# What a list scheduler charges for one pass of a split product beside its columns

## The chip, the cores and the metric

The kernel runs on one core of one Trainium2 chip. The metric is the device time of one execution in microseconds (us). The engines are TensorE (PE; its weight loads are listed as PEld), VectorE (DVE), ScalarE (ACT), GpSimd (POOL) and SyncE (SP), which issues all DMAs of the work described here from one queue, in order. Each engine executes its own instructions in the order in which the program was written out.

## The reference

The input is `q`, `k`, `v` (4 batches, 12 heads, 448 positions, 64 columns each, float32) and six weight matrices. What is computed:

```
attn = softmax(causal(q @ k^T / 8)) @ v          # per batch and head, 448 x 448 scores
x    = attn as 1792 tokens x 768
h    = ((x @ w1) * (x @ w2)) @ w3                # w1, w2: 768 x 1024, w3: 1024 x 1024
x2   = h @ w_out                                 # 1024 x 768
h2   = x2 @ w_in                                 # 768 x 2048
out  = (h2 - tanh(h2)) @ w_out2                  # 2048 x 768
```

## The kernel before

**Split products.** Every large product is computed with both operands split into a high part (rounded to the matmul's format `fp32r`) and a low part (the rest). One step over 128 rows of the contraction is three matmuls into the same PSUM tile: high x low, low x high, high x high. They stand in `gemms` (lines 411, 412 and 413), and one such triple is called a split product here, each of its matmuls a pass. The 896 tokens of a half are worked in two blocks, of 384 and of 512 columns (`BLOCKS`); a 128-column tile of weights is the stationary operand. `w3 @ w_out` is multiplied first (`product`, 384 columns in each pass), so that the bilinear layer is followed by one projection.

**Stages.** The first half of the tokens is batches 0 and 1, the second half batches 2 and 3. `attention` (first half) works 12 pairs of heads: scores (L488), masked minimum (L459, DVE), exponentials (L501, ACT), transposes of the probabilities (L513), their evacuation to SBUF (L267), the product with `v` (L541), the transposed reciprocals (L548), scaling and splitting (L552, L554, L267, L270). `turned` (second half) does the same in another layout (scores L657, product with `v` L683). Beside both run the conversions of the weights (`convert`: load L295, then L304, L314, L317, L321, the high part by a copy L267, the low part by a subtraction L270, the store L327), the product `w3 @ w_out`, and the bilinear layer and the projection of the first half. After the attention come the bilinear layer and the projection of the second half, beside the rest of the conversions, and then the last two layers for both halves (`Second`), with weight tiles fetched (L375) from the scratch that the conversions stored: 768-column tiles into the ring `hl` of three buffers, 512-column tiles into the ring `w`.

**What sets the order.** The program is written out by a list scheduler, `Plan`, when the kernel is built. Each piece of work is a generator (a flow) that asks for an engine and a duration, for a buffer of a ring, or for an event. `Plan.run` keeps the time at which each engine comes free (`free`), takes among all flows the request that can start first (then the lower rank, then the one that was ready first), adds its charge to the engine's time, and lets the flow emit its instructions there. A request may name several engines (`[act(n), dve2(n)]` for a copy, `[pool(n), dves(n)]` for a subtraction); then the one that would end first is taken, with VectorE handicapped by 1.5 us (1.0 us after the attention). The charges are the small functions at lines 198 to 233: `act`, `dve`, `pool`, `pe`, `wide`, `dma`.

All large products of a stage come from one flow with rank `FILLER` = 1000, one after the other; the attention's flows have ranks from 0 up. An attention step that asks for PE and whose last step was on another engine is treated as ready 0.5 us (`MARGIN`) later than it is. So products are placed on PE until an attention step is due. The ends of all requests also decide when evacuations, conversions and DMAs are placed on their engines.

`pe` is called in three places: for a split product, `pe(n, 3)` with n = 384 or 512 (L410); for the transposes of the probabilities, `pe(112, count, 112)` (L508); and for the transposes of the reciprocals, `pe(112, 4, 128)` (L546). The scores and the products with `v` are charged by `wide` or by a constant.

Of the kernel before, what the change touches and what calls it, by code (L numbers as in the profile page):

```python
# [219 lines left out]


def pe(n, passes=1, m=P):
    return "PE", passes * max(n / 2400 + 0.017, 0.107 if m > 112 else 0.096)


def wide(n, count):
# [9 lines left out]
def body(ctx: ExitStack, tc: tile.TileContext, qkd, vd, vd4, w12, w3t, wo, w_in, wo2, out):  # L236
# [161 lines left out]
    def gemms(ring, n, products):  # L398

        bufs = []  # L400
        for _ in products:
            bufs.append((yield ring))
        last = len(products[0][2]) - 1
        for k in range(last + 1):
            for buf, (w, x, needs, finish) in zip(bufs, products):
                for e in needs[k]:
                    yield e
                (wh, wl), (xh, xl) = w(k), x(k)
                ps = buf.t[:, :n]
                yield pe(n, 3)  # L410
                PE.matmul(ps, wh, xl, start=k == 0, stop=False)  # L411
                PE.matmul(ps, wl, xh, start=False, stop=False)  # L412
                PE.matmul(ps, wh, xh, start=False, stop=k == last)  # L413
                if k == last:
                    latest[0] += 1e-6
                    plan.spawn(finish(buf), latest[0])
# [15 lines left out]
    def attention(at, aps, x_a):  # L432
# [37 lines left out]
        def pair(n):  # L470
# [34 lines left out]
            for ring, js in zip(r_pt, ((0,), (1,), (2, 3))):  # L505
                pt = yield ring
                ps = yield r_att
                yield pe(CH, 2 * sum(NCH - j for j in js), CH)  # L508
                for e in range(2):
                    o = 0  # L510
                    for j in js:
                        for i in range(j, NCH):
                            PE.transpose(ps.t[:CH, e, o:o + CH], p[:, e, OFF[i] + j * CH:OFF[i] + (j + 1) * CH],  # L513
                                         ident[:CH, :CH])
                            o += CH
                pts.append(pt)
                events.append(Event())
                plan.spawn(evac(ps, pt, o, events[-1]), rank)
# [24 lines left out]
            for x in pts + [v]:  # L543
                plan.done(x)

            yield pe(CH, NCH, P)  # L546
            for i in range(NCH):
                PE.transpose(ps.t[:, 1, i * CH:(i + 1) * CH], rr.t[:, i].rearrange("p e d -> p (e d)"), ident[:CH, :CH])  # L548
# [565 lines left out]
```

## Time and profile before

| | us |
|---|---|
| median of three runs | 1067.23 |
| lowest and highest of them | 1064.9 and 1068.66 |
| the profiled execution | 1062.6 |
| its span, first to last instruction | 1060.8 |
| PE busy in it | 1036.4 |
| ACT busy, DVE busy, POOL busy | 619.4, 643.3, 242.5 |

The mean granted clock of TensorE is 0.997 of full speed (2.4 GHz). Busy time is the union of an engine's instructions; a matmul's duration in the timeline includes the time that it spends in the pipeline, so the pace of a run of matmuls is read from the distance between their starts. Idle time before an instruction is given in brackets with what ended it.

### The profile page before, as it was taken

The numbers are of one execution on the slowest core, as the hardware profiler recorded it, in microseconds if no ns is written. First come the engines' busy times: TensorE is split into PE (matmuls) and PEld (weight loads), VectorE is DVE, ScalarE is ACT, GpSimd is POOL, SyncE is SP. The second block draws the span as 40 slices with busy tenths as digits, with TensorE's granted clock in tenths as the row PEclk, the third lists the DMA queues.
The fourth block names the chain that finished last, engine by engine and source line by source line (L and its number), as shares of the span: only waits on it lengthen the run. The fifth ranks groups of instructions, "written<-read, shape, count | busy, mean of one in ns | idle before, by whom it ended". The sixth has DMA issues, their size and how long they took to land.

```text
span 1060.8 us, 19813 instructions
## 1 busy us (share of the span) xinstructions
PE 1036.4 (98%) x7680; PEld 899.3 (85%) x7680; DVE 643.3 (61%) x1316; ACT 619.4 (58%) x1353; POOL 242.5 (23%) x188
## 2 busy tenths in 40 slices
PE   5799999999999999999999999999999999999998
PEld 3577788778888989888998989899888988988987
DVE  7886556667665466656565377384756655474742
ACT  6997868788776243433432488573736556553620
POOL 3542131222223400124532022121111111121210
PEclk8999999999999999999999999999999999999999
DMA  7674449877764798999998333233333543233124
GB/s 265 205 215 161 121 149 315 298 255 253 251 223 159 295 366 301 347 323 319 354 326 300 142 118 119 90 129 109 109 110 117 167 140 115 92 120 117 44 87 155
DMA packets 72318, 209.03 MB, mean 197 GB/s; under 512 B 6113, under 2 KB 21473, under 8 KB 70689
## 3 DMA queue, kind: packets, MB, share of 16 engines
q1 hardware_dynamic: 72224, 207.77, 57.0%
q8 instruction: 60, 0.98, 0.4%
q14 instruction: 34, 0.27, 0.1%
HBM read 155.45 MB, written 52.30 MB: 196 GB/s over the span
## 4 chain that ended last, share of the span: by engine, by line
PE 91%; ACT 3%; DMA 2%; DVE 2%; issue 1%; POOL 0%; SPq 0%; ACTq 0%; DVEq 0%
PE mm L411 28%; PE mm L413 27%; PE mm L412 27%; PE pv L683 3%; PE sc L657 2%; PE att L541 1%; DMA raw<-w3t 1%; ACT p L501 1%; PE att L488 1%; PE att L513 1%; ACT pt L267 1%; ACT raw L304 1%; DVE p L459 1%; DMA qk<-qkd 1%; DVE t L321 0%
## 5 line engine op out<-in xcount | busy, mean ns | idle before, releaser
L411 PE MATMUL mm<-x,hl 128*128 128x384 f32 (+1 forms) x768 | 282.1, 367 | 0.0
L413 PE MATMUL mm<-x,hl 128*128 128x384 f32 (+1 forms) x768 | 278.8, 363 | 0.0
L412 PE MATMUL mm<-x,hl 128*128 128x384 f32 (+1 forms) x768 | 278.6, 363 | 0.0
L270 POOL TENSOR_TENSOR g<-g 128x384 fp32r<-128x384 f32 (+1 forms) x64 | 76.7, 1199 | 371.1 <-ACT g L267 371.1
L411 PEld LDWEIGHTS mm<-x,hl 128*128 128x128 f32 x768 | 144.1, 188 | 18.7 <-issue 2.0
L413 PEld LDWEIGHTS mm<-x,hl 128*128 128x128 f32 x768 | 144.1, 188 | 15.3
L412 PEld LDWEIGHTS mm<-x,hl 128*128 128x128 f32 x768 | 144.2, 188 | 14.7
L413 PE MATMUL mm<-g,w 128*128 128x384 f32 (+1 forms) x384 | 139.6, 364 | 0.0
L412 PE MATMUL mm<-g,w 128*128 128x384 f32 (+1 forms) x384 | 139.4, 363 | 0.0
L411 PE MATMUL mm<-g,w 128*128 128x384 f32 (+1 forms) x384 | 139.1, 362 | 0.0
L897 DVE SCALAR_TENSOR_TENSOR g<-r,g 128x512 f32<-128x512 f32 (+1 forms) x192 | 124.7, 659 | 20.4 <-ACT r L888 17.6
L888 ACT ACTIVATE r<-sq,cst 128x384 f32<-128x384 f32 (+1 forms) x192 | 123.6, 666 | 8.0 <-DVE g L897 8.0
L411 PE MATMUL mm<-g,hl 128*128 128x384 f32 (+1 forms) x320 | 116.3, 363 | 2.1 <-POOL g L270 2.1
L413 PE MATMUL mm<-g,hl 128*128 128x384 f32 (+1 forms) x320 | 113.0, 353 | 0.0
L412 PE MATMUL mm<-g,hl 128*128 128x384 f32 (+1 forms) x320 | 112.9, 353 | 0.0
L881 DVE SCALAR_TENSOR_TENSOR g<-sq,mm 128x384 f32<-128x384 f32 (+1 forms) x64 | 39.6, 619 | 109.2 <-ACT th L879 108.6
L314 DVE TENSOR_SCALAR t<-raw 128x512 uint32<-128x512 uint32 (+1 forms) x80 | 52.3, 654 | 69.6 <-DMA raw<-wo 39.1
L875 ACT ACTIVATE sq<-mm 128x384 f32<-128x384 f32 (+1 forms) x64 | 34.7, 543 | 92.5 <-PE mm L413 92.4
L304 ACT ACTIVATE raw<-raw 128x512 uint32<-128x512 uint32 (+1 forms) x80 | 63.9, 799 | 33.7 <-DMA raw<-wo 16.3
L270 POOL TENSOR_TENSOR hl<-t,hl 128x512 fp32r<-128x512 f32 (+1 forms) x32 | 52.1, 1635 | 134.0 <-ACT hl L267 99.1
L321 DVE CUSTOM_DVE_ANT_0 t<-raw,t 128x1024 uint16<-128x1024 uint16 (+1 forms) x80 | 75.1, 938 | 6.7 <-ACT raw L304 0.2
L412 PEld LDWEIGHTS mm<-g,w 128*128 128x128 f32 x384 | 72.1, 188 | 8.0
(81 smaller groups left out, 1599.0 us busy)
## 6 DMA issues: line engine op xcount, KB each, us to landing
hl<-sci SPq DMA_DIRECT2D x32, 768.0 KB, 4.6
w<-sco SPq DMA_DIRECT2D x48, 512.0 KB, 3.5
raw<-w SPq DMA_DIRECT2D x16, 768.0 KB, 5.7
sc<-hl SPq DMA_DIRECT2D x16, 768.0 KB, 4.4
raw<-w_in SPq DMA_DIRECT2D x16, 768.0 KB, 6.7
hl<-scp SPq DMA_DIRECT2D x12, 1024.0 KB, 6.5
hl<-sc SPq DMA_DIRECT2D x16, 768.0 KB, 7.0
raw<-wo SPq DMA_DIRECT2D x24, 512.0 KB, 6.7
```

Of the source, the lines that this page charges most:

```text
L270: (V if eng == "DVE" else G).tensor_tensor(out=out, in0=in0, in1=in1, op=ALU.subtract)
L304: A.activation(out=u, in_=u, func=AF.Copy, scale=2.0 ** -29)
L314: V.tensor_scalar(out=t, in0=raw[:, :n, 1], scalar1=3, scalar2=0x3FFFFFF8, op0=ALU.logical_shift_left, op1=ALU.bitwise_and)
L321: V.tensor_tensor(out=t, in0=t, in1=raw[:, :n, 0], op=ALU.add)
L411: PE.matmul(ps, wh, xl, start=k == 0, stop=False)
L412: PE.matmul(ps, wl, xh, start=False, stop=False)
L413: PE.matmul(ps, wh, xh, start=False, stop=k == last)
L683: PE.matmul(ps.t[e * D:(e + 1) * D, a, have[0] * 32:P], v.t[r, kb, e], x, start=kb == 0, stop=kb == block(a, 4 - 1))
L875: A.activation(out=sq, in_=h, func=AF.Square)
L881: V.scalar_tensor_tensor(out=g, in0=sq, scalar=LEAD, in1=h, op0=ALU.mult, op1=ALU.mult)
L888: A.activation(out=rk.t[:, :n], in_=sq, func=AF.Square, bias=cst[:, k:k + 1])
L897: V.scalar_tensor_tensor(out=g, in0=rk.t[:, :n], scalar=QUAD[k][1], in1=g, op0=ALU.add, op1=ALU.mult)
```

## The change

One constant of one charge is edited. For a request of `passes` matmuls with `n` columns, `pe` takes the columns at 2400 per us and adds 0.014 us for each matmul instead of 0.017 us; the lower bounds of 0.107 us (over 112 rows) and 0.096 us are as before.

```diff
 def pe(n, passes=1, m=P):
-    return "PE", passes * max(n / 2400 + 0.017, 0.107 if m > 112 else 0.096)
+    return "PE", passes * max(n / 2400 + 0.014, 0.107 if m > 112 else 0.096)
```

No instruction's operands, no buffer and no flow is edited.

## Rows read from the trace of the kernel before

**Rows 1.** The page: span, and the busy time and share of each engine.

```profile
span 1060.8 us, 19813 instructions
...
PE 1036.4 (98%) x7680; PEld 899.3 (85%) x7680; DVE 643.3 (61%) x1316; ACT 619.4 (58%) x1353; POOL 242.5 (23%) x188
```

**Rows 2.** Stretch, length, busy us of PE, PEld, DVE, ACT, POOL; clock, DMA, GB/s.

```profile
0.00:50.00 50.00, 33.59 (x204) 22.91 (x206) 40.94 (x101) 40.64 (x97) 23.94 (x24) 0.93 0.71 242
50.00:100.00 50.00, 46.41 (x332) 36.18 (x330) 37.36 (x107) 45.05 (x119) 16.42 (x12) 1.00 0.64 201
100.00:200.00 100.00, 99.00 (x1015) 81.72 (x1012) 58.79 (x179) 75.16 (x206) 22.83 (x16) 1.00 0.62 198
200.00:600.00 400.00, 400.00 (x3865) 347.47 (x3864) 236.58 (x478) 206.37 (x468) 102.54 (x72) 1.00 0.81 287
600.00:1000.00 400.00, 400.00 (x1991) 359.88 (x1990) 246.12 (x416) 241.38 (x448) 71.74 (x60) 1.00 0.34 113
1000.00:1061.00 61.00, 57.37 (x284) 51.13 (x282) 23.49 (x40) 10.80 (x20) 5.01 (x4) 1.00 0.35 115
```

**Rows 3.** Waits of PE, whole span: us in total, times, longest us.

```profile
PE att L488 <- DMA qk<-qkd: 7.4, 1, 7.4
PE att L513 <- ACT p L501: 4.9, 4, 2.2
...
PE mm L411 <- POOL g L270: 2.1, 2, 1.8
```

**Rows 4.** Line 411 alone: stretch, length, PE and PEld busy (x split products).

```profile
0.00:50.00 50.00, 5.23 (x12) 2.54 (x12) 0.93 0.71 242
50.00:150.00 100.00, 24.92 (x68) 12.80 (x68) 1.00 0.52 161
150.00:350.00 200.00, 82.88 (x221) 41.41 (x221) 1.00 0.72 247
350.00:1061.00 711.00, 424.42 (x1172) 219.86 (x1171) 1.00 0.53 185
```

**Rows 5.** Timeline of PE around one run of products: start us, us, instruction.

```profile
160.35 0.44 PE L411 MATMUL mm<-g,hl 128*128 128x384 f32 x1
160.63 0.34 PE L412 MATMUL mm<-g,hl 128*128 128x384 f32 x1
...
163.41 0.34 PE L413 MATMUL mm<-g,hl 128*128 128x384 f32 x1
163.68 1.19 PE L657 MATMUL sc<-qk 64*128 64x448 f32 x8
```

**Rows 6.** Chain of waits, first 110 us, shares by line.

```profile
by line: DMA raw<-w3t 12.3%; ACT p L501 12.3%; PE att L488 6.8%; ACT pt L267 6.4%; ACT raw L304 6.2%; DVE p L459 5.8%; issue 5.4%; DMA qk<-qkd 5.2%; DVE t L321 4.4%; DVE t L317 4.3%; DMA raw<-wo 4.0%; PE att L541 3.7%; PE att L513 3.5%; ACT
```

**Rows 7.** SP queue: waits; weight fetches of 430 to 530 us; two issues.

```profile
SPq L375 <- PE mm L413: 458.1, 101, 11.7
...
SPq L327 <- POOL hl L270: 57.2, 10, 8.0
...
hl<-sc SPq DMA_DIRECT2D x12, 768.0 KB, 7.2
...
442.01 0.52 SPq L375 DMA_DIRECT2D hl<-sc  x1
...
449.23 0.52 SPq L375 DMA_DIRECT2D hl<-sc  x1
```

**Rows 8.** Timeline of the tail: the last addition.

```profile
1057.41 0.56 DVE L931 TENSOR_TENSOR acc<-mm,acc 128x384 f32<-128x384 f32 x1 [1.42 <-PE mm L413]
```

**Rows 9.** Timeline of PE in the start, idle time before in brackets.

```profile
16.90 0.98 PE L513 MATMUL att<-ident,p 112*112 112x112 f32 x8 [2.23 <-ACT p L501]
...
40.24 0.44 PE L411 MATMUL mm<-g,hl 128*128 128x384 f32 x1 [1.80 <-POOL g L270]
...
40.96 2.11 PE L541 MATMUL att<-pt,v 112*64 112x448 f32 x16
```

**Rows 10.** One stretch of the start: busy us of each engine, clock.

```profile
19.00:23.00 4.00, 4.00 (x22) 3.68 (x23) 3.15 (x11) 3.48 (x7) 1.83 (x1) 0.50 0.81 269
```

## The prediction

> **What bounds the kernel now.** I read the shares of the engines first. TensorE (PE) is busy for 1036.4 us of a span of 1060.8 us, so all its idle time together is 24.4 us; VectorE and ScalarE are at 61% and 58% [rows 1]. The view by stretches then says where those 24.4 us lie: 16.41 us in the first 50 us, 3.59 us in the next 50, 1.00 us from 100 to 200 us, none from 200 to 1000 us, and 3.63 us after 1000 us [rows 2]. In the first 100 us ScalarE is the busiest engine, with 85.7 us against PE's 80.0 us and VectorE's 78.3 us; from 200 us on PE alone is full.
>
> Busy is not peak, so the pace has to be read too. From 600 to 1000 us PE begins 1991 passes, 200.9 ns each; products there alternate between blocks of 384 and 512 columns, in the mean 448 columns, which at the granted clock of 1.00 (the 2.4 GHz level) are 186.7 ns. So a pass costs its columns and 14.2 ns. In the mixed stage a run of sixteen 384-column passes takes 163.41 - 160.63 = 2.78 us, 173.8 ns each, which is 160 + 13.8 ns [rows 2, 5]. The chip therefore charges about 0.014 us, the new constant, and nothing in the changed line alters that: each pass on the chip costs what it did.
>
> By the Trainium skill, page "Perfetto Trace Analysis", section "Identifying the Most-Contended Engine", the busy share of matmuls is a poor measure of closeness to the peak, and the share of LDWEIGHTS is the better one. Here that share is 85% [rows 1], so by the page some 161 us of the span would be headroom; the even 200.9 ns per pass over 400 us, with no wait in them, says that no order of the same passes gets at it, and I give a large gain by that rule 1%.
>
> The chain of waits of the first 110 us confirms who rules there: landings of raw weights, ScalarE's exponentials (L501), its evacuations (L267) and its part of the conversion (L304), VectorE's (L317, L321, L459) lead, and products hardly stand in it [rows 6]. PE's own waits are one landing of 7.4 us at the start, four waits for exponentials (4.9 us) and two for POOL's subtraction (2.1 us); the rest are shorter [rows 3].
>
> **The change part by part.** Nothing is added or removed on the chip; what is edited is a number that only the planner sees. A split product is charged three passes: for 384 columns 3 x 0.177 = 0.531 us before and 3 x 0.174 = 0.522 us after, for 512 columns 0.691 and 0.682 us, 9 ns less per product. The transposes of 112 columns go through the same function, but 112/2400 + 0.017 = 0.064 us is under the floors of 0.107 and 0.096 us, so their charge stays. The scores and the products with v are charged elsewhere. So the only effect is through the order on the engines and through the choice of the engine for a copy, a split or a subtraction.
>
> The split products themselves stand in one flow in a fixed order, so PE's order can change in one way only: at each visit of attention the number of products placed before the attention step. The planner lays products end to end until the attention step is due; their number changes only where the time saved so far amounts to a whole product more, so the expected number of changes in a stretch is (products x 9 ns) / 522 ns. The trace has 12 products in the first 50 us, 68 from 50 to 150 us, 221 from 150 to 350 us and 1172 after that [rows 4].
> - First 50 us: 12 x 9 ns = 0.11 us, 0.2 changes. From 50 to 150 us: 0.61 us, 1.2 changes. Only here does PE wait at all, so only here can a change cost or give back idle time. One product more ahead of an attention step fills at most 0.52 us of idle time, or delays the step by as much; I bound one by -0.52 and +0.52 us. With 1.4 changes, and as many again on ScalarE and VectorE (where a step is 0.4 to 0.9 us), that is 2.8 changes of unknown sign: about -1.5 to +1.5 us, and I take 0, since the rows show no side that is preferred.
> - From 150 to 350 us: 221 x 9 ns = 1.99 us, 3.8 changes, but PE has filling all the time (1.00 us idle to 200 us, none from 200 us) [rows 2]. A product before an attention step rather than behind it costs nothing there. What can change is the number of visits: entering a run of products takes (160.63 - 160.35) - 0.174 = 0.106 us extra, leaving it (163.68 - 163.41) - 0.174 = 0.096 us, together 0.20 us [rows 5]. Up to three visits more or fewer give -0.6 to +0.6 us; I take 0.
> - After 350 us the 1172 products are 10.5 us cheaper in the plan, but no attention is left to weave in, so PE's order is the old one. Only ScalarE, VectorE, POOL and the DMA queue are ordered anew. What hides this is slack: a weight tile is fetched into one of three buffers as soon as PE lets one go (the SP queue waits 458.1 us in all for exactly that), at 442.01 and 449.23 us, that is every 7.22 us; the tile is wanted two periods later, 14.4 us after its issue, and lands in 7.2 us [rows 7]. If a conversion's store placed before it in the SP queue waits for POOL as long as the longest in the trace, 8.0 us, the fetch is late by 0.8 us; I take 0 and keep +0.8 us for each of at most three such places, +2.4 us. Below nothing the cost cannot be: there is no idle time to win there.
> - The tail, from the last product to the last output, is one addition of 0.56 us at 1057.41 us and its store [rows 8]. The last block of the fixed flow is the same, so 0, with -0.2 to +0.2 us for the landing of the store.
>
> Sum: 0, with ends of -2.3 (= -1.5 - 0.6 - 0.2) and +4.7 us (= 1.5 + 0.6 + 2.4 + 0.2). The profiled execution took 1062.6 us (its span and 1.8 us around it), so one like it would again take 1062.6 us. It is 4.6 us under the median of the runs shown, 1067.23 us, and 2.3 us under the lowest of them, so I carry the difference of 0 over to the median: 1067.2 us, which I round to 1067.
>
> **The rivals.**
> Faster, through the starved start. The idle time there that isn't the first landing is 16.41 + 3.59 + 1.00 - 7.41 = 13.6 us [rows 2, 3], and a truer PE column may bring the exponentials forward that PE waits for, as at 16.90 us (2.23 us) [rows 9]. For it: these are single waits, and one conversion less in front of an exponential removes one. Against it: only 12 products lie in the first 50 us, so the plan's clock there moves by 0.11 us, and ScalarE, 81% busy there and 90% in the next 50 us, has the same work to do. If the waits for exponentials (4.9 us) and one POOL wait (1.8 us) vanish and a third of that comes back as waits elsewhere, it gains 4.5 us: 1062.7 us.
>
> Slower, through PE's fixed order in the same start. A product that the plan places earlier than the chip converts its weights blocks the attention step behind it. The trace has one such place: at 40.24 us a product waited 1.80 us for POOL's subtraction, and the attention product followed only at 40.96 us [rows 3, 9]. Since ScalarE is nearly full, attention delayed is not caught up before 100 us. The price is 1.8 us for each further place; it decides from the second on (3.6 us), and three would give 1067.2 + 5.4 = 1072.6 us. For it: a plan with shorter products places the next one sooner, and the plan has no knowledge of POOL's delays. Against it: the shift is 9 ns per product against a lag of hundreds. By the Trainium skill, page "TensorE: Matmul & The Clock Gate", section "Step-by-step: what each phase is for", matmuls stay in program order; the row at 40.24 us agrees: what stands behind it starts after it.
>
> No new order where it matters: with 0.2 expected changes in the first 50 us, the first orders may be those of before, and then the 20 us of idle time stay as they are: 1067.2 us, the same number as the forecast by a shorter way.
>
> **How the numbers follow.** About 0.3% (3.2 us) is what a measurement of this kernel tells from no change; three runs of before already span 3.8 us. Chance of the forecast (a difference within 3.2 us, the case without a new order in it): 0.55. Faster, by the refilled start or by the 1% of the page's rule: 0.25. Slower, by blocked products or by late fetches: 0.20. Faster is a little ahead because there are 13.6 us to win, while each loss needs its own place. The forecast's own range is 1064.9 to 1070.4 us (the sum's lower end; the upper one is cut at 3.2 us, beyond which it is the slower case); to leave out no more than 2 in 10 I go to 1060.5 us, 2 us beyond the faster case, and to 1073 us, just beyond three blocked products.
>
> **What would show it.** The pitch in the stretch from 600 to 1000 us must stay at 1991 passes per 400 us, give or take a few records; if it moves, I misread what a pass costs. Idle time from 200 to 1000 us must stay 0; if it doesn't, a fetch or an evacuation came late and the slack was smaller than I take it. Any difference of the span should be found in PE's idle time of the first 100 us (20.0 us now) and in the list of PE's waits; a difference found elsewhere would make the prediction wrong in its reasons, and a start with under 16.8 or over 23.2 us of idle time would make it wrong in its number. The half clock after the gap at 14.7 us (0.50 from 19 to 23 us [rows 10]) should appear again if the first orders are kept.

## The result: slower by 0.57%, and the profile after

Six runs of each kernel: the changed one takes 1073.91 us in the median (1071.53 to 1076.18), the one before 1067.88 us (1064.9 to 1069.81). The ratio is 1.0057, 95% interval 1.0032 to 1.0082, that is 6.0 us more. The profiled execution took 1071.53 us, its span is 1069.8 us at a mean granted clock of 0.991; the one of before took 1062.6 us, span 1060.8 us [rows 1], clock 0.997. The two profiled executions are thus 9.0 us apart, more than the medians; the clock, below, is part of why.

The changed kernel by stretches (from and to, length, then busy us of PE, PEld, DVE, ACT and POOL; then granted clock, DMA share, GB/s), to be held against [rows 2]:

```profile
0.00:50.00 50.00, 33.66 (x187) 22.73 (x188) 39.34 (x101) 38.92 (x94) 22.11 (x24) 0.88 0.71 242
50.00:100.00 50.00, 47.44 (x323) 35.21 (x323) 37.19 (x104) 45.35 (x120) 17.93 (x13) 0.95 0.54 173
100.00:200.00 100.00, 97.71 (x917) 81.46 (x913) 57.49 (x177) 75.08 (x204) 20.92 (x15) 1.00 0.63 200
200.00:600.00 400.00, 397.40 (x3943) 344.01 (x3943) 238.25 (x475) 206.65 (x469) 105.75 (x75) 1.00 0.82 287
600.00:1000.00 400.00, 400.00 (x1992) 359.98 (x1991) 239.32 (x408) 236.82 (x440) 69.47 (x58) 1.00 0.35 115
```

Three things are to be seen. The pace from 600 to 1000 us is that of before, 1992 passes against 1991. From 200 to 600 us, where there was no idle time, there are now 2.60 us (0.76 us before 350 us, at L683, and 1.84 us after). And in the first 100 us PE is idle for 18.9 us, less than before (20.0 us), but it begins 510 instructions instead of 536, at a clock of 0.88 and 0.95 instead of 0.93 and 1.00.

Waits of PE in the changed kernel (us in total, times, longest), against [rows 3]:

```profile
PE att L488 <- DMA qk<-qkd: 7.4, 1, 7.4
PE att L513 <- ACT p L501: 5.5, 4, 2.4
PE mm L411 <- POOL g L270: 3.7, 3, 1.8
PE att L488 <- ACT pt L267: 2.9, 4, 1.1
PE pv L683 <- issue: 2.0, 2, 1.2
```

**Where the 9 us of the profiled pair lie.** The end of the first attention and the products begun by then (timeline row of its last L548, and the stretch up to its end for line 411 alone), kernel before:

```profile
150.85 0.60 PE L548 MATMUL att<-ident,rr 112*128 112x112 f32 x4
```

```profile
0.00:151.40 151.40, 30.33 (x81) 15.53 (x81) 0.98 0.58 187
```

and the changed kernel:

```profile
151.68 0.60 PE L548 MATMUL att<-ident,rr 112*128 112x112 f32 x4
```

```profile
0.00:152.20 152.20, 27.77 (x72) 14.11 (x72) 0.94 0.53 173
```

The change is 0.83 us later there with nine products fewer, worth 9 x 0.522 = 4.7 us: 5.5 us behind. At the last product with v (341.14 us before, 347.50 us after, 288 products begun in both) it is 6.4 us behind, and at the end 9.0 us. So 5.5 us come from the first attention, 0.9 us from the second, 2.6 us from the stretch after it. (That stretch has 1.84 us of idle time in three waits; each costs some 0.28 us more than its idle time, as the starts around the longest show, below.)

**The late wait.** The last split of the second half's bilinear layer, kernel before (ACT and POOL of the timeline; g is the split that the projection reads, cvo a weight's conversion):

```profile
537.37 0.51 ACT L267 CAST g<-asb 128x384 fp32r<-128x384 f32 x1 [2.65 <-DVE asb L801]
537.96 1.01 POOL L270 TENSOR_TENSOR g<-asb,g 128x384 fp32r<-128x384 f32 x1 [1.64 <-ACT g L267]
538.36 0.62 ACT L267 CAST cvo<-t 128x512 fp32r<-128x512 f32 x1 [0.47 <-DMA sco<-cvo]
539.06 1.30 POOL L270 TENSOR_TENSOR cvo<-t,cvo 128x512 fp32r<-128x512 f32 x1
```

and the changed kernel:

```profile
545.23 0.62 ACT L267 CAST cvo<-t 128x512 fp32r<-128x512 f32 x1 [3.20 <-DMA sco<-cvo]
...
545.76 0.51 ACT L267 CAST g<-asb 128x384 fp32r<-128x384 f32 x1
545.93 1.28 POOL L270 TENSOR_TENSOR cvo<-t,cvo 128x512 fp32r<-128x512 f32 x1 [2.29 <-ACT cvo L267]
...
546.40 0.34 PE L413 MATMUL mm<-g,hl 128*128 128x384 f32 x1
...
547.17 1.18 POOL L270 TENSOR_TENSOR g<-asb,g 128x384 fp32r<-128x384 f32 x1
...
548.40 0.44 PE L411 MATMUL mm<-g,hl 128*128 128x384 f32 x1 [1.65 <-POOL g L270]
...
548.68 0.34 PE L412 MATMUL mm<-g,hl 128*128 128x384 f32 x1
```

The planner has put the conversion ahead of the split on both engines. The conversion waits 3.20 us for a store to let its buffer go, the split stands behind it on ACT and again on POOL, and PE waits. From 546.40 to 548.68 us two passes take 2.28 us in place of 0.35 us, so the wait costs 1.93 us, of which 1.65 us are idle.

**The clock.** One stretch of the start, columns as above, of before, then of the changed kernel:

```profile
38.00:56.00 18.00, 12.80 (x99) 8.48 (x96) 16.53 (x38) 17.97 (x50) 9.56 (x5) 1.00 0.67 224
```

```profile
38.00:56.00 18.00, 14.22 (x76) 9.85 (x72) 12.34 (x29) 15.98 (x45) 9.41 (x5) 0.72 0.57 196
```

Both kernels have the same waits just before it: PE waited 1.80 us to 40.24 us before [rows 9] and 1.79 us to 40.20 us after. Before, the clock stayed at the 2.4 GHz level (1.00) afterwards; after, it was at the 1.2 GHz level for some 10 of the 18 us (0.72), and the attention product that took 2.11 us at 40.96 us [rows 9] took 3.80 us:

```profile
40.93 3.80 PE L541 MATMUL att<-pt,v 112*64 112x448 f32 x16
```

### The profile page after: what moved, and what is told of

Same layout as the page of the kernel before. It is cut to its first block, busy times and chain, and to the rows that moved or that the text cites. A ratio compares the mean times of both kernels' runs of the same rounds, so it can differ in the third digit from the quotient of the medians.

```text
span 1069.8 us, 19814 instructions
## 1 busy us (share of the span) xinstructions
PE 1042.5 (97%) x7680; PEld 902.8 (84%) x7680; DVE 642.7 (60%) x1312; ACT 621.1 (58%) x1355; POOL 243.5 (23%) x190
## 4 chain that ended last, share of the span: by engine, by line
PE 87%; DMA 5%; ACT 3%; DVE 3%; issue 1%; POOL 1%; SPq 0%; ACTq 0%; DVEq 0%
PE mm L411 26%; PE mm L413 25%; PE mm L412 25%; PE pv L683 3%; PE sc L657 2%; DMA raw<-wo 2%; DMA raw<-w3t 1%; PE att L541 1%; PE att L513 1%; PE att L488 1%; ACT p L501 1%; DMA raw<-w_in 1%; DMA sco<-cvo 1%; DVE t L317 1%; DVE p L459 1%
```

## The experiments

Ratios are to runs of the kernel before on the same chip, with 95% intervals; the median of before differs from chip to chip (1066.40 to 1067.88 us), so rows are compared by their ratios. Idle is PE's from 350 to 600 us in the one profiled execution.

| run | charge: first attention / second / rest | edit beside it | median us | ratio | idle us |
|---|---|---|---|---|---|
| before | 0.017 / 0.017 / 0.017 | | | 1 | 0 |
| changed | 0.014 / 0.014 / 0.014 | | 1073.91 | 1.0057 (1.0032 to 1.0082) | 1.84 |
| stage_late | 0.017 / 0.017 / 0.014 | | 1069.62 | 1.0025 (1.0008 to 1.0042) | 1.42 |
| stage_att | 0.014 / 0.014 / 0.017 | | 1073.67 | 1.0065 (1.0045 to 1.0085) | 2.26 |
| stage_first | 0.014 / 0.017 / 0.017 | | 1074.48 | 1.0073 (1.0059 to 1.0087) | 1.19 |
| after_dve7 | as changed | last split on VectorE | 1073.17 | 1.0064 (1.0049 to 1.0080) | 2.84 |
| c012 | 0.012 throughout | | 1071.01 | 1.0049 (1.0028 to 1.0071) | 0.57 |
| c016 | 0.016 | | 1068.56 | 1.0012 (0.9995 to 1.0029) | 1.12 |
| c0175 | 0.0175 | | 1071.39 | 1.0035 (1.0016 to 1.0053) | 2.87 |
| c02 | 0.020 | | 1073.72 | 1.0066 (1.0040 to 1.0092) | 3.67 |
| after_flip | as changed | other block first | 1070.97 | 1.0033 (1.0020 to 1.0046) | 1.71 |
| after_rings | as changed | eight PSUM tiles | 1071.14 | 1.0046 (1.0028 to 1.0064) | 2.70 |
| after_both | as changed | both | 1068.34 | 1.0013 (1.0002 to 1.0024) | 0 |
| before_both | as before | both | 1065.83 | 0.9983 (0.9964 to 1.0001) | 0 |
| first_both | 0.014 / 0.017 / 0.017 | both | 1072.16 | 1.0036 (1.0019 to 1.0054) | 0 |
| turned_both | 0.017 / 0.014 / 0.014 | both | 1065.90 | 0.9990 (0.9972 to 1.0009) | 0 |
| c0175_both | 0.0175 | both | 1067.18 | 0.9996 (0.9977 to 1.0015) | 0 |
| c02_both | 0.020 | both | 1069.52 | 1.0034 (1.0010 to 1.0058) | 0 |
| best_again | as before | both | 1066.80 | 0.9992 (0.9972 to 1.0012) | 0 |
| warm | as before | both, and filled waits | 1062.68 | 0.9952 (0.9934 to 0.9970) | 0 |

**Which stage loses.** The charge became a variable that is set at two points of the build, so that the orders up to such a point are exactly those of the kernel with the same charge:

```diff
-    return "PE", passes * max(n / 2400 + 0.017, 0.107 if m > 112 else 0.096)
+    return "PE", passes * max(n / 2400 + PASS[0], 0.107 if m > 112 else 0.096)
...
-        plan.run(xa["over"])
+        plan.run(xa["over"]); PASS[0] = 0.017       # end of the first attention
...
-    cv.__exit__(None, None, None)
+    cv.__exit__(None, None, None); PASS[0] = 0.014  # end of the second
```

stage_late. 

> The charge is 0.017 us until both attentions are over and 0.014 us from there on, so that every engine's order is that of before until about 345 us. Theory 'late stall' (the new charge after the attention places POOL's subtractions so that the last split of the bilinear layer comes late): PE idles or stalls about 2 us between 460 and 560 us, as it did after the change (2.3 us), and the time is before plus 2 us. Theory 'start' (all of the loss lies in the order of the first 200 us): same as before, within 1 us, and no wait of PE for POOL after 350 us. Theory 'half clock' (the loss is time at the lower clock level in the first 60 us): same as before where the mean granted clock is the same.

stage_att. 

> The charge is 0.014 us until both attentions are over (there the order is that of the changed kernel) and 0.017 us from there on. Theory 'start': all of the loss stays, before plus 6 us. Theory 'late stall': the loss is smaller by its 2.3 us, before plus 3 to 4 us, with no wait of PE for POOL after 350 us. Theory 'half clock': before plus 3 us, with a mean granted clock of 0.99 against 0.995 or more of before, and once the half-clock time is taken off nothing is left.

stage_first. 

> The charge is 0.014 us in the first attention (to about 152 us) and 0.017 us from there on. Theory 'start': before plus 5 us, since the first 150 us hold nearly all of the loss. Theory 'late stall': before plus 2 to 3 us. Theory 'half clock': as with the charge kept low in both attentions, before plus 3 us at a clock of 0.99.

The new charge after the attention alone costs 2.7 us (1.0025), with the kind of wait expected:

```profile
PE mm L411 <- POOL g L270: 2.8, 2, 1.8
...
PE mm L411 <- DVE asb L801: 0.5, 1, 0.5
```

Of the 2.8 us, 1.0 us is after 350 us, and so is the 0.5 us. In the first attention alone it costs 7.8 us (1.0073). The parts do not add up to the whole, and with the old charge after 345 us the late idle time did not go (2.26 us in stage_att). So neither theory stands as it was put: waits after 350 us are in the profile of every order here that differs by then, whatever charge is used there, until the late stage gets slack (below).

stage_late has the order of before up to 345 us, and its profiled execution prices the clock there. It ends the first attention 3.3 us later than before with the same 81 products begun:

```profile
154.18 0.60 PE L548 MATMUL att<-ident,rr 112*128 112x112 f32 x4
```

```profile
0.00:154.80 154.80, 30.54 (x81) 15.66 (x81) 0.96 0.56 183
...
38.00:56.00 18.00, 14.22 (x76) 9.89 (x72) 12.54 (x29) 15.09 (x41) 8.21 (x5) 0.72 0.59 199
```

The clock in the stretch from 38 to 56 us is that of the changed kernel, 0.72. So 3.3 us is what one execution of the old order lost to the clock, by chance. In this pair of executions some 2.2 of the 5.5 us are then left for the order of the first attention, an estimate from single executions; more profiles, under "What is left", put it higher. In the medians the clock's part is smaller: the runs of before have a mean clock of 0.994, the six of the changed kernel 0.9915, and in a straight-line fit within the runs of each kernel 1 us more at the lower level went with 0.34 us. (1 - 0.9915) x 2 x 1072 is 18 us at that level against 13 us, so about 1.8 us of the 6.0 us, an estimate. This part may go with the order: over all 61 runs of the eight kernels with 0.014 us in the first attention the mean clock is 0.9925, over the 128 runs of before taken beside the experiments 0.9939.

**Taking away the one late wait.**

```diff
-        sub((yield [pool(n), dves(n)]), lo, x, hi.bitcast(F32))
+        sub((yield dves(n) if on_dve else [pool(n), dves(n)]), lo, x, hi.bitcast(F32))
```

> The changed kernel (0.014 us everywhere), with the subtraction of the bilinear layer's last products of the second half fixed on VectorE, where the changed kernel has it on POOL behind a weight's subtraction; all else before 520 us is the changed kernel's. Theory 'late stall': PE's wait of 1.7 us for POOL before 548 us is gone and the time is 2 us under the changed kernel, before plus 4 us. Theory 'start' and theory 'half clock': the wait is gone as well, but it was hidden or is replaced by another, and the time stays at the changed kernel's, before plus 6 us.

The time stayed, and the idle time did not shrink (2.84 us against 1.84 us). The last split is waited for again, 1.3 us, now on VectorE. Choosing another engine only moved the wait; the split was late because of what stood ahead of it, on ACT:

```profile
547.31 0.62 ACT L267 CAST cvo<-t 128x512 fp32r<-128x512 f32 x1 [2.17 <-DMA sco<-cvo]
547.84 0.51 ACT L267 CAST g<-asb 128x384 fp32r<-128x384 f32 x1
```

The other long wait, 1.4 us for an asb at 471.8 us, lies ahead of the edit. The changed kernel has it at the same place in the same order, 0.16 us long, and after_flip (below) 1.3 us long. So the length of these waits differs from execution to execution.

**Is it the charge, or any new order?** Only the constant differs.

> The charge is 0.0175 us, half a thousandth above before. Its order is that of before for about the first 100 us on every engine. Theory 'the charge itself' (a charge nearer to the chip's 0.014 costs time, and one farther away saves some): before, or up to 1 us less. Theory 'any new order loses' (the order of before is a rare good one, without a wait after 200 us, and every other draw of the planner has its waits): before plus 1 to 4 us, with some idle time of PE between 350 and 600 us.

> The charge is 0.020 us, as far above before as the change is below it. Theory 'the charge itself': faster than before by some us, or at least not slower (1062 to 1067 us). Theory 'any new order loses': before plus 3 to 8 us, like the changed kernel.

> The charge is 0.016 us, a third of the way to the changed kernel. Theory 'the charge itself': a third of the loss, before plus 2 us. Theory 'any new order loses': before plus 3 to 8 us, without regard to how small the step is.

> The charge is 0.012 us, below what the chip shows. Theory 'the charge itself': more loss than at 0.014 us, before plus 10 us. Theory 'any new order loses': before plus 3 to 8 us, no more than the changed kernel.

The theory of the charge itself falls: 0.0175 and 0.020 us, on the other side, lose 0.35% and 0.66%, and 0.012 us loses no more than 0.014 us. 0.016 us cannot be told from before. Each has idle time after 350 us, the largest c02:

```profile
PE mm L411 <- DVE asb L801: 2.4, 2, 1.3
PE mm L411 <- POOL g L270: 1.3, 1, 1.3
```

**Giving the late stage slack.** Two edits. The projection of the second half begins with the block that the bilinear layer did not finish last; and that layer takes its PSUM tiles from the two rings (eight tiles) instead of the ring of two:

```diff
-            xa["yb"] = yield r_x2
+            xa["yb"] = yield r_x2; turn_at[0] ^= 1
...
-            plan.set(ends)
+            turn_at[0] ^= 1; plan.set(ends)
...
-                yield from gemm(r_mm, n, w, xk, [[xr[b][k] ...
+                yield from gemm(r_mm if tiles is jobs_12 else next(rings), n, w, xk, [[xr[b][k] ...
```

> The changed kernel with one edit: the projection of the second half begins with the block of 512 tokens, not with the block of 384 that the bilinear layer has just finished, so that the last split has 4 us more before it is read (and back to the old sense after the projection). Theory 'late stall by the last split': PE's wait for POOL (1.7 us) before the second pair of the projection is gone, the small one for VectorE's asb (0.3 us) stays: 1.8 us under the changed kernel, before plus 4 us. Theory 'any order, the loss is in the start': no wait there either, and the time unchanged within 1 us of the changed kernel.

> The changed kernel with one edit: the bilinear layer of the second half takes its PSUM tiles from both rings (eight tiles) and not from the ring of two. Theory 'late stall by two tiles': the waits on asb (0.3 and 0.2 us near 470 and 528 us) go, the wait for POOL's last split stays: 0.5 us under the changed kernel. If the plan also reads further ahead with eight tiles, up to 2 us under it.

> The changed kernel with both edits (projection begins with the other block; eight PSUM tiles for the bilinear layer of the second half). No wait of PE between 350 and 600 us. If the late waits are 2.3 us of the loss, 2 to 2.5 us under the changed kernel, before plus 3.5 to 4 us; what is then left is the start's and the clock's.

> The kernel before with both edits. It has no wait of PE after 200 us, so nothing is to be had: same as before within 0.5 us, by every theory. If it is slower by 2 us or more with idle time of PE after 350 us, an order changed there loses even with more slack, and the slack was not what kept the wait away.

Each edit alone removes its own wait and leaves the other (after_flip: 1.7 us for asb; after_rings: 2.7 us for POOL's split). Together they remove all idle time from 200 to 1000 us, and the loss shrinks from 0.57% to 0.13%: 1068.34 us. That is 4.7 us by the ratios, more than the 2.6 us that the profiled execution showed. One execution is only a sample of these waits; and on the kernel before, with no late wait to remove, the same edits gave 0.9983, and 0.9992 when it was run again (0.9 to 1.8 us, neither clear of 1).

**What is left.**

> The charge is 0.014 us in the first attention and 0.017 us after it, with both late edits (projection begins with the other block, eight PSUM tiles for the bilinear layer of the second half). If what is left of the loss sits in the order of the first attention: as the changed kernel with both edits, before plus 1 us, and no wait of PE after 350 us. If it sits in the second attention: as the kernel before with both edits, before minus 2 us.

> The charge is 0.017 us in the first attention and 0.014 us after it, with both late edits. The first 150 us have the order of before on every engine. If the rest of the loss sits in the first attention: as the kernel before with both edits, before minus 2 us (1065.5 to 1066.5). If it sits in the second: before plus 1 us.

> The charge is 0.0175 us throughout, with both late edits. If the late waits made the charge of 0.0175 us slower than before: within 1 us of the kernel before with both edits, that is before minus 2 to minus 1 us, and no wait of PE after 350 us (it had 2.9 us). If any new order loses in the start as well: before plus 1 us or more.

> The charge is 0.020 us throughout, with both late edits. Its late waits were 3.7 us; without them before plus 1 to 3 us, the rest being the start's (and a pass at the lower clock level near 220 us). If other waits take their place, it stays at before plus 6 us.

turned_both and after_both differ in the charge of the first attention alone: 0.9990 and 1.0013, so by the ratios that order costs 2.5 us, though the intervals overlap. With the old charge there the new one after it shows no cost once the late stage has slack. c0175_both shows the same from the other side: its 0.35% are gone with the slack (0.9996). c02 loses half with the slack and keeps half, by ratios whose intervals overlap. first_both missed what was expected: 0.36% slower than before, 2.5 us more than after_both by the ratios, with no late idle time; its profiled execution had 3.0 us of waits at L683 and the lower clock level again near 198 us, and which of its orders makes that I did not take apart.

What the order of the first attention costs shows in the place where it first differs. Before, a product stands behind the attention product (L541):

```profile
49.47 1.57 PE L488 MATMUL att<-qk 64*112 64x448 f32 x8
...
53.29 2.11 PE L541 MATMUL att<-pt,v 112*64 112x448 f32 x16 [0.98 <-DVE st L459]
...
56.47 0.42 PE L411 MATMUL mm<-g,hl 128*128 128x384 f32 x1
```

With 0.014 us it stands ahead of it; in after_both, whose rows just ahead agree with those of before within 0.02 us:

```profile
49.45 1.57 PE L488 MATMUL att<-qk 64*112 64x448 f32 x8
...
54.89 0.44 PE L411 MATMUL mm<-g,hl 128*128 128x384 f32 x1 [2.35 <-POOL g L270]
55.61 3.57 PE L541 MATMUL att<-pt,v 112*64 112x448 f32 x16
59.11 0.77 PE L548 MATMUL att<-ident,rr 112*128 112x112 f32 x4
```

The product waits 2.35 us for POOL's subtraction of its weights, and the attention product behind it starts 2.3 us later than before. It then runs at the lower clock level (0.57 from 56 to 60 us), and L548, at 55.33 us before, comes 3.8 us later with one product more done. In the changed kernel's own profile this wait is hidden: the clock had made PE late already, and the subtraction was done when PE came to the product:

```profile
53.50 2.73 PE L488 MATMUL att<-qk 64*112 64x448 f32 x16
56.23 0.44 PE L411 MATMUL mm<-g,hl 128*128 128x384 f32 x1
```

The seven other profiles with 0.014 us in the first attention have the wait at that place, 1.3 to 2.4 us long, and so has c012 (2.35 us); no profile with 0.017 us there has it. Counted as for the profiled pair (end of the last L548, 0.522 us for each product fewer), the eight profiles with 0.014 us are 4.2 to 6.8 us behind before at the end of the first attention; with 0.017 us turned_both, before_both, best_again and stage_late are 0.3, 1.6, 2.2 and 3.3 us behind. The means, with before itself, are 5.5 and 1.5 us, so in the profiles the new order costs some 4 us there, the lower clock that follows the wait included.

**Pricing the clock.** Ten matmuls with zero weights ahead of the product that waits to 40.2 us, and fourteen transposes of the identity ahead of the transposes that wait to 46.7 us; the plan does not know of them:

```diff
+        for _ in range(10 if steps[0] == 9 else 0):
+            PE.matmul(ps, zero, x(0)[0], start=False, stop=False)
...
+                    for _ in range(14 if n == 2 and js == (0,) and e else 0):
+                        PE.transpose(ps.t[:CH, 1, :CH], ident[:CH, :CH], ident[:CH, :CH])
```

> The kernel before with both late edits, and in PE's waits near 38.4 to 40.2 us and 46.6 to 48.1 us ten matmuls with zero weights and fourteen transposes of the identity, uncharged in the plan, so that the order of all else is kept. If idle time in those waits is what lets the granted clock fall to the 1.2 GHz level between 40 and 55 us: no such stretch there, a mean clock of 0.996 or more, and 1.5 to 3 us under the kernel before with both edits (about 1063.5 us). If the clock falls for another reason: the stretches stay and the time is the same or up to 1 us longer.

> The kernel before with both late edits once more (projection of the second half begins with the other block; eight PSUM tiles for its bilinear layer). If its 1.8 us under the kernel before were real: before minus 1 to 2 us again, ratio 0.998. If they were chance: before, ratio 1.000.

warm takes 1062.68 us, 0.9952 of before, the one version here that beats both kernels. Its waits are filled and the clock stays up:

```profile
38.11 2.01 PE L403 MATMUL mm<-g,zero 128*128 128x384 f32 x10
...
44.81 1.50 PE L519 MATMUL att<-ident 112*112 112x112 f32 x14
```

```profile
38.00:56.00 18.00, 15.85 (x120) 11.39 (x117) 16.47 (x38) 17.87 (x50) 9.65 (x5) 1.00 0.65 222
```

Its runs have a mean clock of 0.997 against 0.993 to 0.994 of the same order without the filling, and it is 3.2 to 4.1 us faster than that. best_again, at 0.9992, decides neither way whether the two edits alone gain on the kernel before.

## Why the prediction was wrong

- The pace of the chip: right. A pass costs what it did, and the changed line acts through order alone. (One reading is off without effect: the last stretch of [rows 2] ends 0.2 us behind the span, so the idle time after 1000 us is 3.4 us and not 3.63 us.)
- "After 350 us": one of the two steps that failed. I took 0, because PE's order there is fixed and the weight fetches have 7 us of slack. But that was the slack of the fetches alone. The waits came from two places that I had not looked at: the two PSUM tiles of the bilinear layer, held until VectorE has read them, and the last split, read seven products (3.7 us) after its own product ends and placed behind a conversion. Measured: 2.6 us in the profiled pair, 2.7 us by stage_late (0.9 to 4.5 us), 4.7 us by after_both. I had allowed up to 2.4 us for it, but for late fetches, and as an unlikely end.
- "From 50 to 150 us", -1.5 to +1.5 us: the other step, mis-sized. I bound one changed place by the length of a product, 0.52 us. But a product placed earlier delays the step behind it by the wait for its own operand: at the first changed place 2.3 us in after_both, and 3.8 us with the lower clock level that followed. I also counted changed places (2.8) as if the rest of the order stayed. The first 50 us do have the old order, as expected; at 56.2 us the first product changes places, and others follow. The cost of this order was 2.2 us (profiled pair against stage_late), 2.5 us (after_both against turned_both, by ratios) and some 4 us in the means of the profiles.
- That a new order is as likely to gain as to lose: wrong, and the error behind both. The order of before had no wait from 200 to 1000 us in its profile and had nothing to gain there; the eight other orders without the slack edits (the changed one, the three by stages, the four by other charges) have ratios of 1.0012 to 1.0073, seven of them clear of 1, and none gains.
- The slower rival, a product blocked in the start: it came, at one further place, though the changed kernel's own profile hides it. The wait to 40.2 us is the same (1.79 and 1.80 us); the further one, near 55 us, is 1.3 to 2.4 us long in the seven other profiles of this order. I had priced it well, 1.8 us, but in the sum I used 0.52 us for the same event, and I let the rival decide only from the second place on. With the late waits beside it one place was enough. The late waits have the same mechanism, in-order engines with a late step ahead, on ACT and POOL and at 546 us.
- The faster rival did not come: the waits for exponentials are 5.5 us, against 4.9 us.
- What would show it wrong: the test that idle time from 200 to 1000 us stays 0 named the late fault (2.60 us, of which 1.84 us after 350 us). The test by the idle time of the first 100 us (18.9 us, within the 16.8 to 23.2 us that I gave) was blind to the loss in the start, which stands in the profiled pair as busy time at the lower clock.
- The half clock: I expected it where it had been seen. That the same order may or may not draw it near 40 to 55 us, for 3.3 us, was not in the range.

Open: how much of the lower clock of the six runs of the changed kernel (1.8 us by the fit) the new order draws, and how much is chance, is not settled; and the waits for "issue" at L683 near 195 us (2.0 us, 1.0 us more than before) were not taken apart.

## What to carry to other kernels

A schedule that has been found without a wait need not be a mean draw: here eight of eight re-sorted orders were no faster, the one with a truer model among them. So forecast such an edit as a loss of the size of the waits that the schedule lacks, until slack has been given to the places where they can come, and look, for each stage that shows no idle time, at every short resource (PSUM tiles and last-moment splits, not only DMA) before costing a new order at nothing. Where an engine works in order, price a step that moves forward by the wait for its operand and not by its own length. And compare several executions before a difference of a few microseconds in the start is put down to the program: the clock level alone made 3 us.

## What the runs showed of the hardware that I had not expected

PE's waits of 1.80 us (to 40.2 us) and 1.53 us (to some 48 us) were followed by the 1.2 GHz level in some executions and not in others of the same order: from 38 to 56 us the clock was 0.72 in stage_late, 0.81 in before_both and 1.00 in turned_both and the kernel before. In warm, filling them with matmuls on zeros and transposes kept the level at 2.4 GHz in the profiled execution; the mean clock was 0.996 to 0.998 in each of its eleven runs (0.990 to 0.997 without the filling), and it was worth 0.3 to 0.4%.

Not all time at the lower level costs. From 16 to 28 us the clock was 0.72 before and after the change and 0.86 in stage_late, and the transposes that wait for the exponentials start at 30.95, 30.91 and 30.98 us all the same. So a mean clock over the whole span gives only an estimate of what the clock costs.
